# Emptying the two q banks of a quad: each bank by one engine, instead of both banks by both engines in crossed order

## The chip, the cores and the metric

One core of one Trainium2 chip runs the whole program. The metric is device time in microseconds (us). Several executions of each kernel are timed. A profile is the trace of one such execution.

## The reference

Two attention blocks read the same x (2048 x 1024) with their own weights and are mixed by a gate. The change touches only block B, whose queries look back at eight keys, two positions apart:

```python
qkv = (x @ wqkv).reshape(B, S, 3, H, Dh)...          # H = 32 heads of Dh = 32
idx = pos[:, None] - off[None, :]                    # off = 0, 2, ..., 14
logits = einsum("bhsd,bhswd->bhsw", q, kg) * scale   # masked where idx < 0
o = einsum("bhsw,bhswd->bhsd", softmax(logits), vg)
return g * a + (1 - g) * b                           # a, b: the two blocks' outputs
```

## The kernel before

Block B's k and q are projected in "quads": four PSUM banks are filled by 64x64 matmuls, which run in groups of four, one for each quarter of TensorE's array. Outputs 0 and 2 are k, outputs 1 and 3 are q, for even and odd positions. A quad has four slots; after slot 2 the two k banks are complete, after slot 3 the two q banks. The next quad needs its own two q banks in its slot 1, so there is about one slot's time to empty them. There are sixteen quads, numbered from 0; two make a block of 128 columns; between their matmuls lie the score and value matmuls of earlier blocks.

```python
if slot >= 2:
    a, b = slot, slot - 2                            # q: a = output 3, b = output 1
    for o, part in ((a, 0), (b, 1), (b, 0), (a, 1)):
        outputs[o][2](banks[o], part)
...
def evacuate(ps, part):
    if which == 0:                                   # k: one copy, ScalarE
        if part == 0:
            nc.scalar.copy(out=kt_[:, par, 512 * hh:512 * hh + 512], in_=ps[:])
    elif part == 0:                                  # q, head slot 0: ScalarE
        nc.scalar.activation(out=qz[:, 0, par, :], in_=ps[:], func=ACT.Copy, scale=qsel[:, 0:1])
    else:                                            # q, head slot 1: VectorE
        nc.vector.tensor_scalar(out=qz[:, 1, par, :], in0=ps[:], scalar1=qsel[:, 1:2], scalar2=None,
                                op0=ALU.mult)
```

`qsel` holds 0/1 factors: each q bank is written twice, each copy with the rows of the other head zeroed. So a bank is read twice, and before it was read once by ScalarE and once by VectorE.

The softmax here doesn't subtract the row's maximum and nothing guards it: scores larger than these inputs give would overflow.

## Time and profile before

| what | before |
|---|---|
| time, three runs | 472.9 us (472.75 to 473.04) |
| TensorE busy in the attention part (216 to 360 us) | 143.95 of 144 us |
| VectorE, ScalarE busy there | 95.4 us, 78.3 us |
| reads of q banks | 32 on ScalarE (687 ns), 32 on VectorE (744 ns) |

In the rows of a timeline the first figure is the start in us, the second the length of the (merged) group, then engine, line, operation and operands; a bracket gives the idle time before it and what ended it. The prediction shows an odd and an even quad. The first quad (number 0) is the one with the longest stop; ScalarE, VectorE and TensorE with its weight loads, before:

```profile
223.85 0.69 ACT L426 ACTIVATE qz<-q_ps,qsel 128x512 bf16<-128x512 f32 x1 [0.60 <-PE q_ps L389]
223.96 1.41 DVE L428 TENSOR_SCALAR qz<-q_ps,qsel 128x512 bf16<-128x512 f32 x2
224.74 0.69 ACT L426 ACTIVATE qz<-q_ps,qsel 128x512 bf16<-128x512 f32 x1 [0.21 <-DVE qz L428]
225.15 0.11 PEld L389 LDWEIGHTS <-WqB 64*64 64x64 bf16 x1
225.48 0.84 PE L389 MATMUL q_ps<-xT,WqB 64*64 64x512 bf16 x12
225.48 0.36 PEld L389 LDWEIGHTS <-WqB 64*64 64x64 bf16 x11 [0.23 <-issue]
```

The weights for the first q matmul are loaded at 225.15, but the matmul starts at 225.48, 0.05 us after ScalarE's second read ends (224.74 + 0.69 = 225.43), and the other weight loads queue behind it. No view counts this as idle time of PE, as the earlier matmuls' modelled ends cover it.

### The profile page before, as it was taken

What the parts mean: (1) busy time and instruction counts of PE and PEld (TensorE: products, weight loads), DVE (VectorE), ACT (ScalarE), POOL (GpSimd) and SP (SyncE); (2) the same over time, 40 slices, a digit from 0 to 9 for tenths busy, and PEclk for the clock granted to TensorE, in tenths of its full rate; (3) what the DMA queues carried; (4) which work ended last, traced back from release to release, by engine and by line L of the source; (5) the groups of instructions that cost most, each with busy time, mean ns of one, the idle gap of its engine ahead of it and who ended that gap; (6) DMA issues with size and microseconds to landing.
All of it is one profiled execution on the core that took longest, in us unless ns stands there. A gap on an engine that the chain in (4) does not pass through costs nothing.

```text
span 470.8 us, 13145 instructions
## 1 busy us (share of the span) xinstructions
PE 465.1 (99%) x5735; PEld 249.2 (53%) x5765; DVE 277.2 (59%) x600; ACT 169.7 (36%) x274; POOL 15.3 (3%) x30
## 2 busy tenths in 40 slices
PE   8999999999999999999999999999999999999997
PEld 5444444445444444444677677777764444444444
DVE  0586689990319999999567676767670049800000
ACT  1343321112533333334555555555551134221121
POOL 2300000500000000000000000000000000000000
PEclk9999999999999999999999999999999999999999
DMA  8999970000644243527327525432563913211001
GB/s 208 207 237 377 349 254 0 0 1 1 208 141 123 79 143 125 155 97 250 104 55 111 109 48 94 101 88 57 92 167 73 232 59 79 71 53 46 34 33 46
DMA packets 98732, 55.40 MB, mean 118 GB/s; under 512 B 70130, under 2 KB 90610, under 8 KB 98674
## 3 DMA queue, kind: packets, MB, share of 16 engines
q1 hardware_dynamic: 93378, 49.87, 40.6%
q10 hardware_dynamic: 5296, 4.69, 2.9%
q8 instruction: 45, 0.74, 0.7%
q14 instruction: 13, 0.11, 0.1%
HBM read 26.10 MB, written 15.86 MB: 89 GB/s over the span
## 4 chain that ended last, share of the span: by engine, by line
PE 85%; SPq 11%; DMA 2%; DVE 1%; issue 1%; ACT 0%; DVEq 0%
PE q_ps L389 27%; PE d_ps L593 12%; PE e_ps L593 11%; PE g_ps L220 11%; PE p_ps L294 11%; PE p_ps L330 8%; SPq L115 4%; SPq L81 4%; DMA WvB<-in_B_wqkv_dram 2%; PE po L468 2%; PE s2b L446 2%; SPq L94 1%; SPq L119 1%; SPq L98 1%; SPq L89 1%
## 5 line engine op out<-in xcount | busy, mean ns | idle before, releaser
L389 PE MATMUL q_ps<-xT,WqB 64*64 64x512 bf16 x1024 | 69.0, 377 | 0.0
L389 PE MATMUL q_ps<-xT,WkB 64*64 64x512 bf16 x1024 | 68.5, 376 | 0.0
L156 DVE TENSOR_SCALAR e<-e 128x512 f32<-128x512 f32 x64 | 27.1, 423 | 65.9 <-ACT e L155 65.9
L294 PE MATMUL p_ps<-WvB,xT 128*128 128x512 bf16 x250 | 57.3, 379 | 0.4
L169 PE MATMUL pk_ps<-WkA,xT 128*128 128x512 bf16 x251 | 55.2, 379 | 0.8 <-DMA xT<-in_A_x_dram 0.5
L220 PE MATMUL g_ps<-pk,xrow 128*128 128x512 bf16 x251 | 55.2, 379 | 0.3
L451 ACT ACTIVATE PT<-s2b 128x928 bf16<-128x928 f32 (+4 forms) x40 | 34.1, 854 | 45.2 <-PE s2b L446 45.2
L453 DVE TENSOR_TENSOR PT<-PT,mask 128x928 bf16<-128x928 bf16 (+4 forms) x40 | 23.6, 590 | 35.9 <-ACT PT L451 35.9
L330 PE MATMUL p_ps<-WqA,xT 128*128 128x512 bf16 x188 | 43.0, 379 | 0.2
L593 PEld LDWEIGHTS <-pqT 128*128 128x128 bf16 x272 | 26.0, 98 | 29.7 <-issue 0.4
L593 PEld LDWEIGHTS <-OBT 128*128 128x128 bf16 x272 | 26.0, 98 | 29.4
L169 PEld LDWEIGHTS <-xT 128*128 128x128 bf16 x256 | 25.0, 98 | 30.8 <-DMA xT<-in_A_x_dram 0.8
L220 PEld LDWEIGHTS <-xrow 128*128 128x128 bf16 x256 | 25.0, 98 | 30.2
L294 PEld LDWEIGHTS <-xT 128*128 128x128 bf16 x256 | 24.8, 98 | 30.2 <-issue 0.7
L389 PEld LDWEIGHTS <-WkB 64*64 64x64 bf16 x1024 | 32.6, 107 | 12.4 <-DMA vd<-tmp 0.2
L389 PEld LDWEIGHTS <-WqB 64*64 64x64 bf16 x1024 | 31.6, 107 | 11.1 <-issue 0.2
L600 DVE TENSOR_SCALAR osb<-e_ps,omg 128x128 bf16<-128x128 f32 x1 | 0.3, 350 | 57.6 <-PE e_ps L593 57.6
L155 ACT ACTIVATE e<-pk_ps 128x512 f32<-128x512 f32 x32 | 18.9, 597 | 40.4 <-PE pk_ps L169 36.1
L299 ACT CAST tmp<-p_ps 128x512 bf16<-128x512 f32 x32 | 18.7, 588 | 36.4 <-PE p_ps L294 32.5
L593 PE MATMUL d_ps<-WoA,pqT 128*128 128x512 bf16 (+1 forms) x133 | 30.7, 369 | 0.2
L593 PE MATMUL d_ps<-WoB,OBT 128*128 128x512 bf16 (+1 forms) x134 | 30.7, 369 | 0.1
L330 PEld LDWEIGHTS <-xT 128*128 128x128 bf16 x192 | 18.8, 98 | 22.7
(63 smaller groups left out, 528.5 us busy)
## 6 DMA issues: line engine op xcount, KB each, us to landing
vd<-tmp SPq DMA_DIRECT2D x16, 264.0 KB
xrow<-in_A_x_dram SPq DMA_DIRECT2D x4, 1024.0 KB
out_dram<-osb ACTq DMA_DIRECT2D x31, 128.0 KB
pqd<-tmp SPq DMA_DIRECT2D x12, 256.0 KB
WvA<-in_A_wqkv_dram SPq DMA_DIRECT2D x2, 1024.0 KB
WoA<-in_A_wo_dram SPq DMA_DIRECT2D x2, 1024.0 KB
WvB<-in_B_wqkv_dram SPq DMA_DIRECT2D x2, 1024.0 KB
WqA<-in_A_wqkv_dram SPq DMA_DIRECT2D x2, 1024.0 KB
```

The lines of the kernel that those rows point to most:

```text
L81: nc.sync.dma_start(out=w[:], in_=src[:, c0:c0 + 512].rearrange("(kt p) n -> p kt n", p=P))
L115: nc.sync.dma_start_transpose(out=xT[:, :, t * P:(t + 1) * P], in_=rows(x, t * P, (t + 1) * P))
L155: nc.scalar.activation(out=e[:], in_=pj[:], func=ACT.Exp)
L156: nc.vector.tensor_scalar(out=e[:], in0=e[:], scalar1=1.0, scalar2=1e-6, op0=ALU.min, op1=ALU.add)
L169: nc.tensor.matmul(pj[:], lhsT=xT[:, kt, t * P:(t + 1) * P], rhs=WkA[half][:, kt, :], start=(kt == 0), stop=(kt == KT - 1))
L220: nc.tensor.matmul(pj[:], lhsT=xrow[:, t, kt * P:(kt + 1) * P], rhs=pk[:, t, half * 512:(half + 1) * 512], start=(t == 0), stop=(t == NB - 1))
L294: nc.tensor.matmul(st["pj"][:], lhsT=xT[:, kt, t * P:(t + 1) * P], rhs=WvB[half][:, kt, :], start=(kt == 0), stop=(kt == KT - 1))
L330: nc.tensor.matmul(st["pj"][:], lhsT=xT[:, kt, t * P:(t + 1) * P], rhs=WqA[half][:, kt, :], start=(kt == 0), stop=(kt == KT - 1))
L389: nc.tensor.matmul(banks[o][64 * j:64 * j + 64, :], lhsT=lhsT(r, kt, j), rhs=rhs(r, kt), start=first and kt == 0, stop=kt == KT - 1, skip_ ...
L451: nc.scalar.activation(out=pt[:, :, 0:W_], in_=s2b[:].rearrange("p a b s -> p (a b) s")[:, :, 0:W_], func=ACT.Exp, scale=SCALE)
L453: nc.vector.tensor_tensor(out=pt[:, :, 0:W_], in0=pt[:, :, 0:W_], in1=mask[:, None, base:base + W_].broadcast_to([P, 4, W_]), op=ALU.mult)
L593: nc.tensor.matmul(st["ps"][:, 0:n], lhsT=lhsT, rhs=W[c0 // 512][:, c, c0 % 512:c0 % 512 + n], start=(side == 0 and c == 0), stop=(side == ...
```

## The change

It takes away the waits between ScalarE and VectorE on one bank. Output 3's bank is now read twice by ScalarE, output 1's twice by VectorE.

```diff
-                            for o, part in ((a, 0), (b, 1), (b, 0), (a, 1)):
-                                outputs[o][2](banks[o], part)
+                            for o, part in ((a, 0), (b, 0), (a, 1), (b, 1)):
+                                outputs[o][2](banks[o], part, o == a)
...
-                def evacuate(ps, part):
+                def evacuate(ps, part, on_act):
...
-                    elif part == 0:
-                        nc.scalar.activation(out=qz[:, 0, par, :], in_=ps[:], func=ACT.Copy, scale=qsel[:, 0:1])
+                    elif on_act:
+                        nc.scalar.activation(out=qz[:, part, par, :], in_=ps[:], func=ACT.Copy,
+                                             scale=qsel[:, part:part + 1])
                     else:
-                        nc.vector.tensor_scalar(out=qz[:, 1, par, :], in0=ps[:], scalar1=qsel[:, 1:2], scalar2=None,
-                                                op0=ALU.mult)
+                        nc.vector.tensor_scalar(out=qz[:, part, par, :], in0=ps[:], scalar1=qsel[:, part:part + 1],
+                                                scalar2=None, op0=ALU.mult)
```

(A second `evacuate`, for eight late copies, takes the new argument and ignores it.)

More of the change, by code (lines that the diff above doesn't have):

```diff
@@ L553, in rhs, with evacuate @@
                     return WqA[half][64 * r:64 * r + 64, kt, :]
-                def evacuate(ps, part):
+                def evacuate(ps, part, on_act):
                     if part == 0:
```

## The prediction

> **What bounds the kernel now.** I read the head of the page, then the chain that ended last, then the attention part alone (216.7 to 357 us: the "quads" that project k and q, at L389), there the waits, and last the timelines of TensorE, ScalarE and VectorE around the end of two quads.
>
> The page's head and its chain:
>
> ```profile
> span 470.8 us, 13145 instructions
> PE 465.1 (99%) x5735; PEld 249.2 (53%) x5765; DVE 277.2 (59%) x600; ACT 169.7 (36%) x274; POOL 15.3 (3%) x30
> ...
> PE 85%; SPq 11%; DMA 2%; DVE 1%; issue 1%; ACT 0%; DVEq 0%
> ```
>
> TensorE carries 85% of the chain. ScalarE and VectorE, the only engines whose work the change touches, carry about 1% together, so their speed matters only where TensorE waits for them. A table of stretches, one line for each block of 128 columns of q and k (two quads and their scores), gives busy us (instructions) of PE, PEld, DVE, ACT and POOL:
>
> ```profile
> 250.12:265.94 15.82, 15.82 (x478) 11.24 (x472) 10.91 (x38) 8.85 (x13) 0.00 (x0) 1.00 0.62 104
> 265.94:281.75 15.81, 15.81 (x477) 11.20 (x472) 10.89 (x38) 8.85 (x13) 0.00 (x0) 1.00 0.43 87
> ```
>
> PE is busy for all of it, at full clock, and each block takes the same 15.81 us. But modelled, overlapping matmul spans can hide a short stall, so I also use start-to-start distances of single matmuls. The projection issues them in groups of four, one per 64x64 quarter of the array; where nothing is late, a group starts 215 to 216 ns after the one before.
>
> The waits in that part:
>
> ```profile
> ACT qz L426 <- ACT kt L424: 6.2, 14, 0.5
> ACT qz L426 <- DVE qz L428: 2.4, 9, 0.3
> ```
>
> The second line is the crossed order at work: ScalarE's second q read waits for VectorE's first (total us, times, longest). The first is ScalarE idling until TensorE finishes q; the change leaves it.
>
> End of an odd quad: ScalarE, VectorE, TensorE, each from its own timeline:
>
> ```profile
> 279.01 0.69 ACT L426 ACTIVATE qz<-q_ps,qsel 128x512 bf16<-128x512 f32 x1 [0.34 <-ACT kt L424]
> 279.97 0.69 ACT L426 ACTIVATE qz<-q_ps,qsel 128x512 bf16<-128x512 f32 x1 [0.27 <-DVE qz L428]
> ```
> ```profile
> 278.52 0.76 DVE L481 TENSOR_TENSOR Ob<-po,rd 128x256 bf16<-128x256 f32 x2
> 279.19 1.40 DVE L428 TENSOR_SCALAR qz<-q_ps,qsel 128x512 bf16<-128x512 f32 x2
> ```
> ```profile
> 280.50 0.40 PE L389 MATMUL q_ps<-xT,WkB 64*64 64x512 bf16 x3
> 280.70 0.63 PE L389 MATMUL q_ps<-xT,WqB 64*64 64x512 bf16 x8
> ```
>
> VectorE comes 0.18 us late because it is still writing Ob; ScalarE's second read waits for it and ends at 280.65. The first matmul of the next quad that needs a q bank starts at 280.70, 0.05 us later. End of an even quad:
>
> ```profile
> 271.01 1.46 ACT L426 ACTIVATE qz<-q_ps,qsel 128x512 bf16<-128x512 f32 x2 [0.55 <-ACT kt L424]
> ```
> ```profile
> 271.00 1.49 DVE L428 TENSOR_SCALAR qz<-q_ps,qsel 128x512 bf16<-128x512 f32 x2
> ```
> ```profile
> 272.79 0.63 PE L389 MATMUL q_ps<-xT,WqB 64*64 64x512 bf16 x8
> ```
>
> Here both engines are done by 272.49, and TensorE comes to those banks at 272.79: 0.3 us to spare.
>
> **What the Trainium skill says.** "PSUM — Partial Sum Buffer", section "PSUM bank collisions raise a hardware error": two engines may not access one bank in the same partitions at once, two reads included, so software must put a wait between them. The trace agrees that such waits are there: in all 16 quads ScalarE's second read starts 0.03 us or more after VectorE's first read of that bank ends. That is why the kernel crossed the order. The same page (its opening notes, on parallel access) says that the two engines read different banks at full bandwidth. The durations fit: 687 ns (ScalarE) and 741 to 752 ns (VectorE) in every quad, whatever the overlap. "Perfetto Trace Analysis", section "Identifying the Most-Contended Engine", warns that matmul busy time does not tell how near TensorE is to its limit; hence the start-to-start distances. "VectorE: DVE Perf Modes", section "The TRN2 errata", gives 215 ns for a 512-column matmul, which is the distance measured here, so the groups run at the array's rate.
>
> **The change part by part.** Outputs 0 and 2 of a quad are k, 1 and 3 are q. k's copies (part 0 only, ScalarE, bank 2 then 0) keep their order, and so do the eight late copies to raw. For q:
>
> Removed: nothing that computes. Before and after, ScalarE does 32 activations of 687 ns and VectorE 32 tensor_scalars of 744 ns; shapes and the 0/1 factors are the same. What goes is the cross waits. Before, bank 3 was read by ScalarE then VectorE, bank 1 by VectorE then ScalarE. Now ScalarE reads bank 3 twice and VectorE bank 1 twice, without waiting for each other.
>
> ScalarE: its two q reads start 0.77 us apart in even quads (271.01 to 271.78) and 0.96 in odd ones (279.01 to 279.97). Without the wait they follow each other; its back-to-back k copies overlap by some 0.11 us (2 x 0.59 in 1.07), so I estimate 0.58 us apart: the second ends 0.2 us earlier in even and 0.4 us earlier in odd quads.
>
> VectorE: starts are 0.73 us apart in even quads (271.00 to 271.73, right after ScalarE's first ends at 271.70) and 0.66 in odd ones, where ScalarE is long done. So 0.66 everywhere; even quads gain 0.07, odd ones nothing.
>
> Release of the banks: now VectorE's second read ends last everywhere. In odd quads that was already 280.59, against ScalarE's 280.65; the last release moves 0.06 us.
>
> On the path: how long does TensorE really stall? From the last k group to the first q group of the next quad, first matmul to first matmul, the seven odd quads of blocks 0 to 6 show 230, 226, 233, 227, 232, 227 and 232 ns instead of 215.5. Excess: 14.5 + 10.5 + 17.5 + 11.5 + 16.5 + 11.5 + 16.5 = 98.5 ns. The 15th quad has no successor of this kind. The even quads after the first show 215 to 216 ns: no stall. The very first quad shows 334, a stall of 118 ns, as no score matmuls lie between; its q reads ended at 225.43 (ScalarE) and 225.37 (VectorE), so only 0.06 us of the 0.118 goes.
>
> Sum: 0.10 + 0.06 = 0.16 us off TensorE's stream. No later slack swallows it, since TensorE is the chain to the end. 472.9 - 0.16 = 472.74, which I give as 472.8.
>
> **The rivals.** (1) The waits named in the profile are the gain: if ScalarE's 2.4 us lay on the path, the time would be 470.5, 0.5% less. Against it: ScalarE has 0% of the chain, and the score exponentials wait 45.2 us for TensorE and not the reverse. Even this stays within 2%. (2) A new wait: bank 1, which TensorE takes first, now hangs on VectorE alone, the fuller of the two engines (59% against 36%). When VectorE is late, TensorE might stall for both reads: with 0.2 us in each of 16 quads, 3.2 us more, 476.1. Against it: VectorE already had to read both banks before either could be reused, and its second read ends no later than now. (3) Unsynchronised reading slows the reads: 10% longer reads would end VectorE's pair 0.15 us later and cost the eight tight quads about 0.05 to 0.1 us each, at most 0.8 us. Against it: the durations are the same in quads that overlap differently. (4) Nothing at all moves: the stalls of 10 to 18 ns are absorbed by how the four quarters drift against each other (the fourth matmul of those groups is only 3 to 4 ns late). Then only the 0.06 us of the first quad remains: 472.84.
>
> **Range and chances.** The runs before spread over 0.29 us, more than the expected gain. The range allows that spread on both sides, and a little for another session: 472.3 to 473.2. For a 2% change 9.5 us would have to move; all bank waits together are 0.22 us, and the whole pairs of reads, were they put serially on TensorE's path, would be 16 x 1.5 = 24 us. Only an unforeseen dependency brings that: 0.01 for slower, 0.005 for faster, 0.985 for within 2%.
>
> **What would show it right or wrong.** The line of ScalarE's qz waiting for VectorE's qz should be gone. ScalarE's q reads should start about 0.58 us apart and VectorE's 0.66 in all quads, at unchanged durations. VectorE's second read should be the last to end, and in odd quads the next q matmul should come about 0.1 us after it and not 0.05, at group distances of 215 to 216 ns; the first quad should keep a stall near 0.06 us. Blocks should stay at 15.8 us. It would be wrong if reads grew longer, if VectorE's first read started later than now, or if a block took other than 15.75 to 15.85 us.

## The result, and the profile after

The changed kernel took 472.40 us (472.29 to 472.97, six runs) against 472.86 us (472.62 to 473.16, six runs). The ratio is 0.9991, with a 95% interval of 0.9978 to 1.0004: the same. A ratio here is the mean time of one kernel's runs over that of the other's in the same rounds, so it is not quite the ratio of the medians. Executions over 1.5% slower than the fastest of the same kernel are left out of the means.

The page's head and chain, after:

```profile
span 471.2 us, 13192 instructions
PE 467.1 (99%) x5765; PEld 270.9 (57%) x5765; DVE 276.6 (59%) x600; ACT 168.0 (36%) x274; POOL 15.4 (3%) x30
...
PE 98%; DMA 1%; DVE 0%; issue 0%; DVEq 0%
```

Two differences from before mislead. The chain gives PE 98% and not 85% with 11% for the SP queue; but the kernel before, traced once more in experiment 1, gave 97% and no SP queue. And this span is longer than before's, because the traced execution was the slowest of its six. Its trace shows why: stops of TensorE's weight loads that waited for nothing the profile shows ("issue"), two near the start and one at 351 us:

```profile
5.83 0.15 PEld L169 LDWEIGHTS <-xT 128*128 128x128 bf16 x1 [0.28 <-issue]
6.26 0.75 PEld L169 LDWEIGHTS <-xT 128*128 128x128 bf16 x4 [0.28 <-issue]
...
350.98 1.00 PEld L389 LDWEIGHTS <-xT 64*64 64x64 bf16 x22 [0.27 <-issue]
```

The quads begin 0.344 us later than in the trace before, and about 0.2 us is lost at 351 us. Taken off its 472.97 us, that leaves 472.43, in line with the other five runs (472.29 to 472.45). None of them came back when this kernel was traced again (experiment 2).

The waits on q reads in the attention part, after:

```profile
ACT qz L426 <- ACT kt L424: 6.0, 14, 0.5
...
ACT qz L426 <- PE q_ps L389: 0.9, 2, 0.6
...
PEld L389 <- DVE qz L429: 0.2, 1, 0.2
```

The wait of ScalarE for VectorE's read (2.4 us in 9 cases) is gone. In its place one TensorE wait for VectorE's read has come to light. The odd quad that answers to the prediction's, then the even one, each by engine:

```profile
279.24 1.27 ACT L426 ACTIVATE qz<-q_ps,qsel 128x512 bf16<-128x512 f32 x2 [0.32 <-ACT kt L424]
279.44 1.40 DVE L429 TENSOR_SCALAR qz<-q_ps,qsel 128x512 bf16<-128x512 f32 x2
280.91 0.64 PE L389 MATMUL q_ps<-xT,WqB 64*64 64x512 bf16 x7
```
```profile
271.24 1.27 ACT L426 ACTIVATE qz<-q_ps,qsel 128x512 bf16<-128x512 f32 x2 [0.53 <-ACT kt L424]
271.24 1.40 DVE L429 TENSOR_SCALAR qz<-q_ps,qsel 128x512 bf16<-128x512 f32 x2
273.01 0.65 PE L389 MATMUL q_ps<-xT,WqB 64*64 64x512 bf16 x7
```

ScalarE's two reads are now one piece of 1.27 us; before they took 1.46 us in the even quad and 1.64 us, with a hole, in the odd one. VectorE's end is now the later one in both, at 280.84 and 272.64. And the first quad:

```profile
224.19 1.26 ACT L426 ACTIVATE qz<-q_ps,qsel 128x512 bf16<-128x512 f32 x2 [0.60 <-PE q_ps L389]
224.30 1.41 DVE L429 TENSOR_SCALAR qz<-q_ps,qsel 128x512 bf16<-128x512 f32 x2
225.70 0.81 PE L389 MATMUL q_ps<-xT,WqB 64*64 64x512 bf16 x9
```

VectorE reads until 225.71, yet TensorE starts its first q matmul at 225.70: that one took ScalarE's bank, free since 225.46. The second starts at 225.763, as a single instruction in the trace, 0.05 us after VectorE's end.

To see what TensorE gained, I measure from the start of the first k weight load of the quads, so that the start-up falls out:

| from the first k weights, us | to the first k weights of the last quad | to its last q weights | to the end |
|---|---|---|---|
| before | 117.051 | 124.891 | 254.148 |
| before, traced again (experiment 1) | 117.060 | 124.901 | 254.158 |
| after | 116.897 | 124.778 | 254.193 (with the 0.2 us stop at 351 us) |
| after, traced again (experiment 2) | 116.897 | 124.779 | 254.019 |

Two traces of one kernel agree within 0.01 us here. The change is worth 0.15 to 0.16 us at the first column's mark, 0.11 to 0.12 at the second's, and 0.13 to 0.14 at the end in the undisturbed traces. Most of the first column's gain, 0.106 us, comes in the first hand-over; each later block of two quads takes 15.803 to 15.808 us and not 15.811 to 15.815, which makes 0.05 us up to the last quad. The first column is marked by the quarter of the array that leads. By the fourth matmul of each group, which comes last, the first hand-over gained 0.062 us: the leading quarter now runs ahead of the others.

### The profile page after: what moved, and what is told of

It is laid out like the page before. It is cut to its first block, busy times and chain, and to the rows that moved or that the text cites. A ratio compares the mean times of both kernels' runs of the same rounds, so it can differ in the third digit from the quotient of the medians.

```text
span 471.2 us, 13192 instructions
## 1 busy us (share of the span) xinstructions
PE 467.1 (99%) x5765; PEld 270.9 (57%) x5765; DVE 276.6 (59%) x600; ACT 168.0 (36%) x274; POOL 15.4 (3%) x30
## 4 chain that ended last, share of the span: by engine, by line
PE 98%; DMA 1%; DVE 0%; issue 0%; DVEq 0%
PE q_ps L389 26%; PE d_ps L594 12%; PE pk_ps L169 12%; PE p_ps L294 12%; PE g_ps L220 12%; PE e_ps L594 12%; PE p_ps L330 9%; PE po L469 2%; PE s2b L447 2%; DMA xT<-in_A_x_dram 1%; PE kv_ps L240 0%; PE w_ps L283 0%; DVE osb L601 0%; DVEq L601 0%
## 5 line engine op out<-in xcount | busy, mean ns | idle before, releaser
L389 PE MATMUL q_ps<-xT,WqB 64*64 64x512 bf16 x1024 | 70.3, 376 | 0.0
L389 PE MATMUL q_ps<-xT,WkB 64*64 64x512 bf16 x1024 | 69.8, 376 | 0.0
L389 PEld LDWEIGHTS <-WkB 64*64 64x64 bf16 x1024 | 40.3, 107 | 7.0 <-DMA vd<-tmp 0.2
L389 PEld LDWEIGHTS <-WqB 64*64 64x64 bf16 x1024 | 39.4, 107 | 5.6 <-DVE qz L429 0.2
L469 PEld LDWEIGHTS <-PT 64*56 64x56 bf16 (+2 forms) x1152 | 30.1, 104 | 4.4
```

The costliest lines, as they stand in the source:

```text
L389: nc.tensor.matmul(banks[o][64 * j:64 * j + 64, :], lhsT=lhsT(r, kt, j), rhs=rhs(r, kt), start=first and kt == 0, stop=kt == KT - 1, skip_ ...
L469: nc.tensor.matmul(o2[64 * h:64 * h + w, par, s_, i, :], lhsT=pt[r, i, o:o + w], rhs=V[r, m, 4 * c + i, :], start=True, stop=True)
```

## The experiments

Eight kernels ran, in two calls with a chip each; all compared correct with the reference. The kernel before took 472.75 us in the first call (eleven runs) and 472.71 us in the second (nine runs).

### 1. The kernel before against itself

No edit.

> The kernel before against itself, in five rounds: what the timing shows where nothing changed. My theory (the change is worth 0.16 us of TensorE's time, the rest of the 0.4 us measured is scatter between executions, from the first DMAs and from single stops of TensorE's own stream) expects 472.8 us, a difference within 0.3 us either way, and in its trace a start of the projection stage (first weight load of L169's second group) and of the quads that differs by some tenths of a us from the trace before, while the time from the first k group of the first quad to the last q group of the last stays within 0.02 us of 121.56. The rival (the whole 0.4 us is the change) expects differences under 0.1 us here.

Measured: 472.73 us (472.65 to 472.83, five runs), ratio 0.9995 (0.9983 to 1.0007). The quads begin 0.25 us later than in the first trace of this kernel (216.952 against 216.701), and from there to the last q weights 0.010 us separate the two. So the measured time scatters by some tenths of a us between executions of one kernel, while the quads repeat to about 0.01 us; of these two traces' difference in span (470.85 against 471.11 us) the start-up makes 0.25. (The figure of 121.56 us in the expectation is the distance from the first q group to the first group of the last quad's slot 3, another pair of marks than the table's or than the expectation's own words.) A ratio as far from 1 as 0.9995 needs no change of the kernel.

### 2. The changed kernel again

No edit to the changed kernel.

> The changed kernel again, in five rounds on the same chip. My theory expects it 0.1 to 0.3 us below the kernel before (ratio 0.9994 to 0.9998), and from the first to the last hand-over of the quads again about 0.155 us less than in the trace before (0.106 in the first hand-over, 0.005 to 0.011 in each later odd one). The rival, that ScalarE coming free 0.3 us earlier per quad also helps somewhere, expects 0.4 us or more (ratio below 0.9992). The second rival, that nothing at all moved, expects a ratio of 1.0000 within 0.0003.

Measured: 472.56 us (472.40 to 472.99, six runs), ratio 0.9993 (0.9981 to 1.0005). That is 0.19 us below the median of the kernel before, within what my theory expects by the medians; the ratio lies between the 0.9994 of my theory and the 0.9992 of the rival, and the interval also takes in no change at all, so the timings settle nothing. The trace does: 0.154 to 0.163 us less to the last quad's first k weights, as in the first trace of this kernel, 0.103 of it in the first hand-over. The rival of 0.4 us finds nothing in the quads or after them.

### 3. Each bank by both engines, in the same order

```diff
-                            for o, part in ((a, 0), (b, 1), (b, 0), (a, 1)):
+                            for o, part in ((a, 0), (a, 1), (b, 0), (b, 1)):
```
(on the kernel before)

> The opposite of the change: each bank is read by ScalarE and then by VectorE, both banks in the same order (bank 3: ScalarE, VectorE; then bank 1: ScalarE, VectorE), so that the engines do not work side by side on different banks. Same 64 instructions. If TensorE at the hand-over waits just for the end of the last read plus 0.05 us: VectorE's second read ends about 2.12 us after ScalarE's first starts (0.69 + 0.03 + 0.66 + 0.74), TensorE would come without a wait at 1.78 (even), 1.68 (odd) and 1.51 us (first quad), so it stops for 0.39, 0.49 and 0.66 us: 7 x 0.39 + 7 x 0.49 + 0.66 = 6.8 us, less the 0.22 us of stops that the kernel before has: 6.6 us more than before, 479.4 us (478 to 480.5). If the banks' release does not govern TensorE, or if slack later takes it back, it stays within 1 us of the kernel before.

Measured: 479.78 us (479.66 to 479.84), ratio 1.0144 (1.0130 to 1.0157): 7.0 us more. The waits in the attention part (total us, times, longest):

```profile
DVE qz L428 <- ACT qz L426: 8.7, 16, 0.7
PEld L389 <- issue: 8.5, 16, 0.6
```

and an odd quad, VectorE and TensorE:

```profile
282.82 1.41 DVE L428 TENSOR_SCALAR qz<-q_ps,qsel 128x512 bf16<-128x512 f32 x2 [0.46 <-ACT qz L426]
...
283.75 0.38 PE L389 MATMUL q_ps<-xT,WqB 64*64 64x512 bf16 x1
284.28 0.84 PE L389 MATMUL q_ps<-xT,WqB 64*64 64x512 bf16 x11 [0.16 <-DVE qz L428]
```

VectorE starts only when ScalarE's first read is over and ends at 284.23; one q matmul finds a free bank at 283.75, the next comes 0.05 us after VectorE's end. The stops (by the fourth matmul of the group, here and below) are 0.37 us in even quads, 0.46 in odd ones and 0.67 in the first, against 0.39, 0.49 and 0.66 expected. The same 64 instructions in another order cost 1.4%: the release of the q banks does govern TensorE, once it falls behind.

### 4. Each bank read once

```diff
-                        nc.scalar.activation(out=qz[:, part, par, :], in_=ps[:], func=ACT.Copy,
+                        nc.scalar.activation(out=qz[:, part, par, :], in_=ps[:] if part == 0 else mask[:, 0:512], func=ACT.Copy,
...
-                        nc.vector.tensor_scalar(out=qz[:, part, par, :], in0=ps[:], scalar1=qsel[:, part:part + 1],
+                        nc.vector.tensor_scalar(out=qz[:, part, par, :], in0=ps[:] if part == 0 else mask[:, 0:512], scalar1=qsel[:, part:part + 1],
```
(on the changed kernel; wrong, half of q is replaced by mask values. The comparison passed it all the same, so its tolerance does not see this half of q.)

> Wrong on purpose: the changed kernel, but the second piece that each engine writes is made from the mask in SBUF and not from the q bank, so each bank is read once and is free after the first read (about 0.7 us earlier). It is the floor of what any order of these four reads can give. My theory: the changed kernel has no stop left but 0.056 us in the first quad, so this is equal to it within 0.1 us (0.2 us below the kernel before), and in its trace the first hand-over shows 216 ns in all four quarters. If a wait on the q banks were still hidden in the changed kernel, this would be faster than it by 0.5 us or more.

Measured: 472.63 us (472.50 to 472.89, five runs), ratio to before 0.9994 (0.9982 to 1.0006). In the trace the first hand-over takes 216 ns in all four quarters, and the way to the last q weights is 124.698 us, 0.08 us under the changed kernel. To the end of the program it is 254.010 us, 0.01 us under it (254.019), which is no more than two traces of one kernel differ by. The edit does not only free the banks: VectorE's second piece, read from the mask, takes 0.34 us and not 0.74, and ScalarE's 0.71 and not 0.68. With that said, freeing these banks earlier can bring about 0.08 us at the last q weights and nothing measurable at the end, and no larger wait on them is hidden in the changed kernel. The odd hand-overs still show 219 to 220 ns here, with the banks long free: those last 3 to 4 ns are not a wait for a read.

### 5. VectorE's read written first

```diff
-                            for o, part in ((a, 0), (b, 0), (a, 1), (b, 1)):
+                            for o, part in (((b, 0), (a, 0), (b, 1), (a, 1)) if vec_first and slot == 3 else
+                                            ((a, 0), (b, 0), (a, 1), (b, 1))):
```
(on the changed kernel, with `vec_first` true in the quads)

> The changed kernel with the four q reads written in the order VectorE, ScalarE, VectorE, ScalarE: the same reads by the same engines on the same banks. The trace after shows that TensorE's first q matmul of the next quad took ScalarE's bank and only the second VectorE's, against what my prediction said. My explanation: buffers are handed on in the order in which their last read stands in the program, not by their own number. It expects here that the first q matmul takes VectorE's bank: in the first hand-over the first matmul itself comes about 0.05 us after VectorE's second read ends (about 272 to 275 ns after the k group, not 216), with the other three 3 to 4 ns behind it each. The time stays within 0.2 us of the changed kernel. If buffers go by their number, nothing changes in the trace.

Measured: 472.63 us median (472.49 to 475.29, four runs, one of them far off the rest), ratio 1.0011 (0.9989 to 1.0034). The trace is that of the changed kernel: 124.776 us to the last q weights, the first hand-over at 216 ns for the first matmul, the second 57 ns behind it, waiting for VectorE. So my explanation, the order in the program, is refuted. Nor do buffers go by their number: in the built programs outputs 1 and 3 of successive quads lie in PSUM banks 0 and 3, then 3 and 0, after the change, and always in 0 and 3 before it. (The prediction's "bank 1" and "bank 3" are the banks of outputs 1 and 3.) The build hands on first the bank that ScalarE reads. Why is open; that it plans with times of its own, in which ScalarE ends first, would fit, but no run shows it.

### 6. The crossed order with VectorE made late

```diff
+                            if slot == 3:
+                                nc.vector.tensor_reduce(out=delay[:], in_=banks[b][:, 0:384],
+                                                        axis=mybir.AxisListType.X, op=ALU.add)
                             for o, part in ((a, 0), (b, 1), (b, 0), (a, 1)):
```
(on the kernel before; `delay` is a new 128x1 tile)

> The kernel before (crossed order), with VectorE made late: a sum over 384 columns of the q bank that it is to read first[...], put before its two q reads. Estimate with starts 0.44 us apart: VectorE's first read starts 0.44 us later than now, ScalarE's second waits for it and ends 1.91 us after ScalarE's first start in even quads (2.09 odd, 2.02 first), release 0.05 later. TensorE stops for 0.18 us in even, 0.46 in odd quads, 0.56 in the first: 5.0 us, about 4.8 us over the kernel before: 477.7 us (476 to 479). If VectorE's lateness were absorbed, under 1 us.

Measured: 480.13 us (479.71 to 480.30, four runs), ratio 1.0155 (1.0142 to 1.0169): 7.4 us more, outside the range I gave. The waits in the attention part, and the odd quad's ScalarE, VectorE and TensorE:

```profile
ACT qz L430 <- DVE qz L432: 11.4, 16, 0.8
PEld L472 <- issue: 1.3, 7, 0.2
```
```profile
282.53 0.69 ACT L430 ACTIVATE qz<-q_ps,qsel 128x512 bf16<-128x512 f32 x1 [0.34 <-ACT kt L428]
284.01 0.69 ACT L430 ACTIVATE qz<-q_ps,qsel 128x512 bf16<-128x512 f32 x1 [0.80 <-DVE qz L432]
...
282.71 0.55 DVE L406 TENSOR_REDUCE delay<-q_ps 128x1 f32<-128x384 f32 x1
283.17 1.40 DVE L432 TENSOR_SCALAR qz<-q_ps,qsel 128x512 bf16<-128x512 f32 x2
...
284.75 0.80 PE L390 MATMUL q_ps<-xT,WqB 64*64 64x512 bf16 x9 [0.35 <-ACT qz L430]
```

The mechanism is as expected: ScalarE waits for VectorE's first read, and TensorE for ScalarE's second. The sizes were short. ScalarE starts 0.09 us after VectorE's read ends (283.92 to 284.01), not 0.03 to 0.04 us as in the kernel before, so the stops are 0.23, 0.52 and 0.64 us and not 0.18, 0.46 and 0.56. Between the two the trace has a wait instruction of ScalarE's sequencer, as this read now waits for two engines. "Perfetto Trace Analysis", section "Identifying Dependency Chains", says that waits on several engines may be put into such an instruction ahead of the waiting one; that it costs the 0.05 us is my reading, not isolated. The sum itself took 0.55 us, and VectorE's first read started 0.47 us later than before (0.44 estimated). I had also left out the sixteenth hand-over, from the last quad to the late copies (0.52 us here), and the late copies, which also got the extra sum. The stops at the sixteen hand-overs sum to 6.4 us, 6.2 more than before. The late copies with their sum take about 0.3 us longer besides. The rest, some 0.7 us by the traces, is lost inside slot 1, behind the stops. About 0.3 us of it comes straight after each stop, where the second group follows after 239 to 241 ns; the kernel before shows 216 to 226 there, and 240 after its first stop. The other 0.43 us is lost once in each of the seven quads that follow an even one, before the value matmuls (ScalarE, VectorE and TensorE, each from its own timeline):

```profile
276.09 0.55 ACT L455 ACTIVATE PT<-s2b 128x452 bf16<-128x452 f32 x1
276.67 0.41 DVE L457 TENSOR_TENSOR PT<-PT,mask 128x452 bf16<-128x452 bf16 x1 [0.60 <-ACT PT L455]
277.21 0.76 DVE L485 TENSOR_TENSOR Ob<-po,rd 128x256 bf16<-128x256 f32 x2
278.02 0.30 PE L472 MATMUL po<-V,PT 64*57 64x33 bf16 x16
```

ScalarE's exponential of the scores follows its delayed second read, VectorE's mask follows the exponential, and VectorE's reads of the accumulator po end late, at 277.97. The next value matmuls into po start 0.05 us after that, and the groups around them are 393 to 400 ns apart and not 334 as before. (Their weight loads stand idle for 0.18 us each time, line PEld L472 above; about 0.06 of it is lost to the groups.) So a late read of a q bank reaches TensorE by a second path, over what the delayed engine does next.

### 7. The changed kernel with VectorE made late

The same three lines ahead of the changed loop.

> The changed kernel with VectorE late by the same sum. Here only VectorE's second read sets the release, 1.84 us after ScalarE's first start in even quads (2.02 odd, 1.95 first): stops of 0.11, 0.39 and 0.49 us, 4.0 us in all, about 3.8 us over the kernel before: 476.7 us, 1.0 us (0.07 us in each of 15 hand-overs) under the crossed order made late. My theory says so: what the change is worth per hand-over is only the 0.07 us by which ScalarE's delayed read outlasted VectorE's. The rival that ScalarE's freedom is the gain expects the difference to be 0.3 us or more a hand-over, 4 us or more; the rival that depending on VectorE alone is worse expects this one to be slower than the crossed order.

Measured: 477.75 us (477.26 to 479.32, five runs), ratio 1.0113 (1.0097 to 1.0129): 5.0 us more than before, and 2.4 us less than the crossed order made late, by the medians. The same views:

```profile
280.88 1.26 ACT L430 ACTIVATE qz<-q_ps,qsel 128x512 bf16<-128x512 f32 x2 [0.34 <-ACT kt L428]
...
281.53 1.40 DVE L433 TENSOR_SCALAR qz<-q_ps,qsel 128x512 bf16<-128x512 f32 x2
...
282.53 1.08 PE L390 MATMUL q_ps<-xT,WqB 64*64 64x512 bf16 x9
```

ScalarE runs through and has its bank free at 282.15; the first q matmul starts at 282.53 without a stop (220 ns), the others when VectorE's second read ends at 282.93, plus 0.05. The stops are 0.10, 0.38 and 0.515 us, against 0.11, 0.39 and 0.49 expected. With VectorE late the stops are 0.12 to 0.13 us shorter a hand-over than in the crossed order, and not 0.07: VectorE's second read ends 0.12 us before the one that ScalarE has to delay there (2.045 against 2.167 us after ScalarE's first start in odd quads, 1.860 against 1.982 in even ones). But 0.06 us of this is the later start that ScalarE's second read has in experiment 6 (0.094 and not 0.034 us after VectorE's), which the kernel before doesn't have; without it 0.07 us is left, as expected. Another 0.4 us of the difference is the second path of experiment 6: here the groups around the value matmuls are 333 to 335 ns apart. So the 2.4 us is more than the crossed order alone would lose. The rivals: it is not a loss, and not 4 us, but the one that saw a gain in ScalarE's freedom was right for that 0.4 us.

### 8. All four reads on ScalarE

```diff
-                                outputs[o][2](banks[o], part, o == a)
+                                outputs[o][2](banks[o], part, True)
```
(on the changed kernel)

> Both q banks emptied by ScalarE alone, all four reads in a row, no cross wait at all and VectorE relieved of 32 instructions. If the release of the banks governs: fourth read ends 3 x 0.59 + 0.69 = 2.46 us after the first starts, release 2.51; stops of 0.73 (even), 0.83 (odd) and 1.0 us (first): 7 x 0.73 + 7 x 0.83 + 1.0 = 11.9 us, about 11.7 over the kernel before: 484.6 us (482 to 486.5). If the cross waits or VectorE's load were what costs, it would be within 1 us of the kernel before or faster.

Measured: 485.41 us (485.28 to 485.89, four runs), ratio 1.0270 (1.0256 to 1.0284): 12.7 us more. ScalarE and TensorE in an odd quad:

```profile
284.90 2.42 ACT L426 ACTIVATE qz<-q_ps,qsel 128x512 bf16<-128x512 f32 x4 [0.34 <-ACT kt L424]
...
286.79 0.37 PE L389 MATMUL q_ps<-xT,WqB 64*64 64x512 bf16 x1
287.37 0.63 PE L389 MATMUL q_ps<-xT,WqB 64*64 64x512 bf16 x8 [0.20 <-ACT qz L426]
```

The first q matmul comes 0.05 us after ScalarE's third read, the second 0.05 us after its fourth. The stops are 0.66, 0.77 and 0.96 us (0.73, 0.83 and 1.0 expected). There is no cross wait and VectorE has 32 instructions less, yet it is the slowest: working side by side is what matters, not the absence of waits.

No experiment points to a version that beats the changed kernel by more than the 0.08 us of the floor.

## Why the prediction was right

**The bound.** TensorE's stream decides, and in the kernels before and after the hand-over of the q banks is the one place where these reads are seen to touch it; experiments 6 and 8 open a second one, before the value matmuls (396 to 402 ns in experiment 8). Experiments 3, 7 and 8 bear out the first at doses of 5 to 13 us, with stops within 0.07 us a hand-over of those computed beforehand from the ends of the reads. In all of them the matmuls that waited start 50 to 55 ns after the last read of their bank ends.

**The parts.** ScalarE's two starts are 0.585 us apart in every quad (0.58 predicted). VectorE's are 0.65 to 0.67 apart (0.66). The durations did not move: medians of 684 and 742 ns after 687 and 744, so the third rival, slower reads, falls. VectorE's read ends last everywhere, as predicted. The odd hand-overs went from 226 to 233 down to 219 to 220 ns, and the first quad keeps a stop of 56 ns (0.06 predicted), in three of the four quarters.

**The sum.** 0.16 us predicted; 0.154 and 0.163 us to the last quad's first k weights, but 0.11 to 0.12 us where all four quarters are done and 0.13 to 0.14 us at the end. That the first mark meets 0.16 so well is luck: it is made up of about 0.105 us in the first hand-over and 0.05 us in the odd ones, where the prediction had 0.06 and 0.10. The term that was mis-sized is the 98.5 ns of the odd quads. The fourth rival was half right there: adding up excess by first matmuls overstates the gain, as the other quarters had drifted and stopped less; by fourth matmuls the stops of the fifteen hand-overs sum to 0.139 us before and 0.078 after, all of the difference in the first, and the odd ones gain 0.05 us in the group behind them (220 to 226 ns before, 215 to 216 after). The 0.06 us of the first is right by that count. (472.74 was also given as 472.8, where it rounds to 472.7; that changes nothing.) The measured time, 472.40 us and 472.56 us when repeated, lies in the range; its distance from before is no evidence for the size, as experiment 1 shows.

**What was wrong in detail.** First, the second rival's reason, "bank 1, which TensorE takes first, now hangs on VectorE alone": the first matmul takes the bank that ScalarE has read. The risk it names is smaller for that, as one quarter goes ahead. Second, the prediction left out the hand-over from the last quad to the late copies; it went from 226 to 220 ns and is too small to matter there, but it was missed in the estimates for experiments 3, 6, 7 and 8 too. Third, the first q matmul comes 0.06 to 0.08 us after VectorE's end in odd quads, not 0.1: the quarter that leads now runs 23 to 64 ns ahead of the next.

## What to carry to other kernels

In this kernel a wait between the two engines that empty buffers cost what it added to the last release beyond the time at which the consumer came for the buffer, and, when it grew (experiment 6), what it delayed on the waiting engine behind it; the total in a list of waits (2.4 us here) says little (0.13 us). Sharing out whole banks, so that each engine runs through and lets its own bank go, was never worse here: 0.13 us, too little for the timings, and up to 2.4 us with VectorE made late. But keep both engines at work: reading one bank with both engines in turn, or giving all to one, cost 7 and 13 us. Where a gain is below the scatter of the timings, take marks on the bounding engine's stream in two traces of each kernel; these repeated to 0.01 us.

## What the Trainium skill lacked or had wrong

- "PSUM — Partial Sum Buffer" says that two engines' accesses to one bank have to be kept apart, but not what a hand-over costs: here 50 to 56 ns from the end of the last read to the start of a waiting matmul into the bank, and 0.03 to 0.04 us from one engine's read to the other's.
- "VectorE: DVE Perf Modes", section "The TRN2 errata": its cycle table gives, as estimates for 512 columns from PSUM, (120 + 512) / 0.96 GHz = 658 ns on VectorE and (172 + 512) / 1.2 GHz = 570 ns on ScalarE. The trace's durations are 742 and 687 ns; the estimates agree with the distance between starts of instructions that follow each other (0.65 to 0.67 us, and 569 to 587 ns). The section says that the SBUF figure for VectorE is short of a duration, but not so for the PSUM figures, and in this case a buffer came free by the duration.
- "Perfetto Trace Analysis", section "Identifying the Most-Contended Engine", takes the time of all weight loads, summed, over the window as a good measure for TensorE. It does not say how to read that sum where loads of several quarters of the array overlap: here it is 128% of the span, before as after. The profile's own share, the union of their spans, rose from 53% to 57% without any more work, while the four quarters drifted apart (mostly 35 to 38 ns from the first to the fourth matmul of a k or q group before, 79 ns after). Neither is a distance to a limit.
- "Perfetto Trace Analysis", section "Identifying Dependency Chains", names the wait instructions put ahead of an instruction that waits for several engines, but no cost: experiment 6 has 0.09 us with one between two reads, where 0.03 to 0.04 us was seen without.
